# Retention and two feed-forward layers on one core: four edits to who makes the decay table, when the second layer's weights are rounded, and the order of the hand-over between the layers

## The chip, the cores and the metric

The kernel runs on one core of one Trainium2 chip. The metric is the device time of the program in microseconds; the median of the runs is compared. Five engines matter here: TensorE (PE for its matmuls, PEld for the loading of their weights), VectorE (DVE), ScalarE (ACT), GpSimd (POOL), and SyncE (SP), which only issues transfers. Each runs its own instructions in order, and waits for the others by semaphores.

## The reference

All is in float32. With 4 batches, 8 heads, 576 positions and 64 columns a head:

```
scores = scale * q @ k.T
ret    = scores * gamma[h] ** (i - j)   where i >= j, else 0
x      = ret @ v                          # as 2304 tokens x 512
h      = x @ w_in                         # 512 x 2048
P      = a0 + a1*h + a2*h^2 + a3*h^3
Q      = 1 + |b0|*|h| + |b1|*h^2
y      = (P / (Q + 1e-6)) @ w_out         # 2048 x 512
h2     = y @ w2_in
out    = (s * relu(h2)^2 + b) @ w2_out
```

## The kernel before, in words

**Numbers.** The products of the two layers are made of rounded operands (fp32r): each operand is split in a high part and the rest, and each product is three matmuls (`three`, L435): high x low, low x high, high x high.

**Retention** (`retention`). 16 pairs of heads are walked in a hand-written order. For a pair p the loop does, on TensorE: `value_state(p)` (L301), `state(p + 1)` (L289), `value_chunk(p)` (L309) and `scores(p + 2)` (L274). Around them ScalarE copies the state (L292), VectorE adds to it (L293), masks the scores (L278), and multiplies the result by the decay table `odec` (L312); ScalarE and GpSimd split the product x into `xh` and `xl`. The two `pv` tiles in PSUM alternate, so `state(p + 1)` writes where x of pair p - 1 was read from. GpSimd scales v of pair p + 3 (L256). The inputs come over SP's queue, five pairs ahead. The table `odec` has four head pairs; its first 128 columns are loaded, and `decay` (L249) makes the other 448 from them by three multiplications with a power of gamma a row: columns 128, 256 and 64 wide. It is called for head pair 0 at the start, and for 1 to 3 in the loop's rounds 1 to 3.

**Weights.** One tile `raw{kf}` (1 MB, loaded over SP's queue) holds a block of w_in and of w_out, as 64-bit numbers. It is rounded by `w_round`: one ScalarE instruction (`wm`, L139) and three of VectorE (L140, L142, L145), and split by `w_split` (ScalarE's cast of the high part, GpSimd's subtraction for the low). In the retention the first three tiles are rounded step by step (L177 to L185). There are 16 tiles a layer (numbers 0 to 15 and 16 to 31), and only a few buffers: from tile 15 on two `raw` buffers alternate, so a tile is loaded when the one two before it has had its last reader. For layer two, GpSimd also makes four sums of two tiles (`s_sums`, L635 to L638), which are then split (`s_split`, L646 and L588) and written to DRAM.

**Layer one** is cut in 72 units, numbers 0 to 71. A unit has its own h (one PSUM bank, 12 matmuls of 512 columns, or 24 of 256), then `rational` (L481): a chain of some six ScalarE, five VectorE and two GpSimd instructions that ends in the split gate `gh` and `gl` (or `gx`, for both), then its output product `o` (12 matmuls, L525). `emit_cuts` puts the rounding of tiles 3 to 15 between units; tiles 16 and 17, the first of layer two, are rounded by `first_cuts` (L920), one step a unit, from the unit at which `free_at[NF - W_BUFS + 1]` is reached.

**Layer two** is done in quads of two tiles (`quad`). The first quad of a pass has four full products (`hs00`, `hs01`, `hs11`, `hs10`, and a tail `ht`); the others use seven products of block sums in place of eight. The sums of token blocks are made by GpSimd's adding transfers (`x_sum`, L603) and split by `x_split` (L612, L588). Output products of the quad before (`p`, `out2`) are taken from a list between the products by `fill(n)`. The first contribution of each is copied from PSUM to `acc` (L726), by VectorE and ScalarE in turn; later ones are added by VectorE (L728).

**What sets the order.** In the retention every instruction is pinned in the order of the code. In the layers a scheduler sets each engine's order at build time; `behind(...)` holds an instruction back until those named have been issued, and `fill` sets how many output products stand between two products.

Of the kernel before, what the change touches and what calls it, by code (L numbers as in the profile page):

```python
# [14 lines left out]
AF = mybir.ActivationFunctionType  # L15
ALU = mybir.AluOpType
# [13 lines left out]
W_BUFS = 5  # L30
# [9 lines left out]
W_FIRST = 3  # L40
# [4 lines left out]
def retention_ffn_kernel(ctx, tc, a, b, s2, b2, w, qkv, maskv, gdec, out):  # L45
    nc = tc.nc
# [5 lines left out]
    NF = w.shape[0] // 2  # L52
# [30 lines left out]
    w_raw = {}  # L83
# [13 lines left out]
    def next_load(eng=nc.sync, pin=free):  # L97
        if w_ahead:
            loads[:] = loads[-1:] + [w_load(w_ahead.pop(0), eng, pin)]
# [71 lines left out]
    def w_cut_in_halves(kf):  # L171
        pin = tc.keep_in_program_order
        lo, hi = w_words(kf)
        m = wtmp.tile([P, 2 * DM], F32, tag="wm", name=f"wm{kf}")
        t = m.bitcast(U32)
        halves = [slice(DM * x, DM * (x + 1)) for x in range(2)]
        pin(nc.scalar.activation(m, hi.bitcast(F32), AF.Copy, scale=2.0 ** -112))  # L177
        pin(nc.vector.tensor_scalar(lo, lo, 2.0 ** -29, 7.0, op0=ALU.mult, op1=ALU.min))
        yield
        for x in halves:  # L180
            pin(nc.vector.scalar_tensor_tensor(out=t[:, x], in0=t[:, x], scalar=3, in1=lo[:, x],
                                               op0=ALU.logical_shift_left, op1=ALU.bitwise_or))
            yield
        for x in halves:
            pin(nc.vector.scalar_tensor_tensor(out=hi[:, x], in0=hi[:, x], scalar=0x80000000, in1=t[:, x],  # L185
                                               op0=ALU.bitwise_and, op1=ALU.bitwise_or))
            if x.start:
                w_split(kf, True)
                del w_raw[kf]
            yield  # L190
# [6 lines left out]
    def retention(actx):  # L197
# [15 lines left out]
        powers = mv[:, NV:].rearrange("p (k h) -> p k h", k=3)  # L213
# [34 lines left out]

        def decay(hp):  # L249
            for k, (t0, t1) in enumerate(((P, 2 * P), (2 * P, 4 * P), (4 * P, S))):  # L250
                dve(nc.vector.tensor_scalar(odec[:, hp, t0:t1], odec[:, hp, 0:t1 - t0], powers[:, k, hp:hp + 1], None, op0=ALU.mult))

        def scale(p, eng=nc.gpsimd):
            if p < NPAIR:
# [123 lines left out]
                    pass  # L378
        for _ in steps:
            pass  # L380
        next_load()


    def ffn(fctx):
# [66 lines left out]
        NU = len(units)  # L451
# [22 lines left out]
        def behind(*instructions):  # L474

            hold = ExitStack()
            for x in instructions:
                hold.enter_context(tc.issue_after(x.ins))
            return hold
# [227 lines left out]
        def out2(q, j, e, parts=1):  # L707

            t0 = 2048 if j == 2 else 1024 * (q // (NF // 2)) + 512 * j
            es = slice(e * P, (e + 1) * P)  # L710
            k = out_units.setdefault((t0, e), 0)
            n = DM // parts
            for x0 in range(0, DM, n):
                cols = slice(x0, x0 + n)
                ps = ps_o.tile([P, 512], F32, tag="o", name=f"p{16 * q + 4 * j + e}_{x0}")[:, 0:n]
                for i in range(2):
                    if j == 2:
                        g = [x[:, 256 * i:][:, es] for x in gt["q", q, 0, 2]]
                    else:
                        g = [x[:, es] for x in gt["q", q, i, j]]  # L720
                    wf, lf = (t.rearrange("p c f -> p (c f)")[:, cols] for t in w_t[NF + 2 * q + i, 1])
                    for x in three(ps, g, (wf, lf), i == 0, i == 1):
                        pe(x)
                at = acc[:, NC * t0 + e * DM:NC * t0 + (e + 1) * DM][:, cols]
                if k == 0:
                    (nc.vector.tensor_copy if e % 2 else nc.scalar.copy)(at, ps)  # L726
                else:
                    nc.vector.tensor_tensor(out=at, in0=at, in1=ps, op=ALU.add)  # L728
                if k + 1 == NF // 2:
                    nc.sync.dma_start(out=out[t0 + e * P:t0 + (e + 1) * P, cols], in_=at)  # L730
            if e == (3, 3, 1)[j]:
                for i in range(2):
                    g_done(("q", q, i, j))
            out_units[t0, e] = k + 1
# [15 lines left out]
        def quad(q, fills):  # L750
# [49 lines left out]
            if q % (NQ // 2) == 0:  # L800
                while late:
                    late.pop(0)()

                tags = ("hA", "hB", "hG", "hT") if first else ("hA", "hT", "hG", "hB")
                order = ((0, 0), (0, 1), (1, 1), (1, 0)) if first else ((0, 0), (1, 0), (0, 1), (1, 1))
                for n, ((i, j), tag) in enumerate(zip(order, tags)):
                    ps = ps_h.tile([P, 512], F32, tag=tag, name=f"hs{i}{j}")
                    wh, wl = tiles_of(q)[i]
                    for c in range(NC):
                        h, l = both(f"{c // 2 + 1}{j + 1}", pas)  # L810
                        for x in three(ps, (wh[:, c, :], wl[:, c, :]), (h[:, c % 2, :], l[:, c % 2, :]), c == 0, c == NC - 1):
                            pe(x)
                    if not first:
                        split = relu2(("q", q, i, j), ps, True, wait=True)
                        fill((4, 4, 2, 0)[n])
                        done = split()
                    else:
                        done = relu2(("q", q, i, j), ps, True)
                    with behind(*ends, *done):
                        if n == 0:  # L820
                            if first:
                                cut_first()
                            else:
                                x_sum(1, "4")
                        if n == 1 and not first:
                            x_split(pas, "1")
                        if n == (2 if first else 1):
                            x_split(pas, "3")
                    if first:
                        fill(4)  # L830
                    with behind(*ends, *done):
                        if n == 2 and first:
                            x_sum(0, "4")
                            cut_second()
                        if n == 3:
                            with behind(*tail_lo):
                                x_split(pas, "2")
                    ends[:] = done
                if first:
                    tail_in(q)  # L840
                else:
                    with behind(*ends):
                        x_split(1, "4")
                fill(len(fills))
                return
# [3 lines left out]
            last = q == NQ // 2 - 1  # L849

            product(q, 1, hA, True)
            copied = nc.scalar.copy(hB, hA)
            if q == 1:

                with behind(copied):
                    x_split(0, "1")
            while late:
                late.pop(0)()
            n1, n2, n3, n4, n5 = (3, 1, 2, 2, 1) if q == 1 else (2, 2, 2, 2, 1) if first else (2, 1, 1, 2, 2)
            fill(n1)  # L860
            product(q, 2, hA, False)
            split = relu2(("q", q, 0, 0), hA, True, wait=True)
# [52 lines left out]

        sums = ["1", "3", "2", "4"]
        raw_gone = []
        first_rounds = None
        next_cuts = iter(())

        def first_cuts():
            yield from w_round(NF)
            w_split(NF)
            yield
            yield from w_round(NF + 1)

        for u in range(NU):
            emit_in(u)
            if u:
                emit_cuts(u)  # L930
            with behind(*ends):
                next(next_cuts, None)
            rational(u)
            if not items and not cuts and not raw_gone:
                raw_to_g()
                raw_gone.append(u)
            for x in outs_at[u]:
                if x < NU - 3:
                    for e in range(NC):
                        out1(x, e)  # L940
            if final[0:1024].all() and len(sums) > (1 if u == NU - 1 else 2):
                x = sums.pop(0)
                if x in ("1", "3"):
                    x_negate(0, {"1": "11", "3": "22"}[x])
                with behind(*ends):
                    x_sum(0, x)
            if not items and not cuts and first_rounds is None and u + 1 >= free_at[NF - W_BUFS + 1]:
                first_rounds = True
                next_cuts = first_cuts()
        assert first_rounds and sums == ["4"]  # L950
        for _ in next_cuts:
            pass
        rest = [lambda x=x, e=e: out1(x, e, pe) for x in range(NU - 3, NU) for e in range(NC)]
        w_split(NF + 1)
        for x in (NF, NF + 1):
# [90 lines left out]
```

## Time and profile before

| | |
|---|---|
| median of 3 runs | 858.07 us (857.96 to 858.33) |
| the profiled execution | 857.59 us, of which the span of instructions is 855.8 us |
| PE busy | 841.9 us, 98% |
| PEld busy | 713.2 us, 83% |
| DVE busy | 637.6 us, 75% |
| ACT busy | 584.1 us, 68% |
| POOL busy | 397.7 us, 46% |

Times in rows are from the span's start. A row of the timeline has its start, its length, the engine, the line, the operation with its tiles and shapes, how many were merged, and in brackets the engine's idle time before it and what ended that. The retention takes the first 72 us or so, layer one runs to about 473, layer two to the end.

### The profile page before, as it was taken

The page shows a single profiled execution, that of the slowest core. Times are in us where ns is not written, and L with a number is a line of the kernel's source. Part 1 is how long each engine was busy: PE and PEld are TensorE (multiplying, and loading weights), DVE is VectorE, ACT ScalarE, POOL GpSimd, SP SyncE. Part 2 cuts the span into 40 slices and gives each one's busy share as a digit, 9 for nine tenths or more (in the row PEclk, how much of TensorE's full clock was granted, in tenths as well). Part 3 has the DMA queues.
Part 4 walks back from the last instruction along what each step waited for, and adds up shares of the span by engine and source line. Part 5 has one row for each costly group of instructions (what it writes and reads, how often), then busy time and mean ns, then how long its engine had stood idle before and what let it go on. Part 6 is the DMA issues. An engine that isn't in the chain of part 4 may idle for free.

```text
span 855.8 us, 12807 instructions
## 1 busy us (share of the span) xinstructions
PE 841.9 (98%) x4840; PEld 713.2 (83%) x4840; DVE 637.6 (75%) x892; ACT 584.1 (68%) x940; POOL 397.7 (46%) x322
## 2 busy tenths in 40 slices
PE   8999999999999999999999999999999999999998
PEld 7898788888888888888887877888888888888887
DVE  5986887788798879788799977887878554444444
ACT  1236997886787878788789776876668666544443
POOL 3687675465566755557457443442236221111100
PEclk9999999999999999999999999999999999999999
DMA  9992110111102101101003476455779985544302
GB/s 342 402 359 100 49 50 1 50 50 49 50 2 99 50 2 50 49 1 50 2 1 80 118 246 208 152 170 208 246 249 371 244 243 161 158 148 149 123 0 99
DMA packets 39181, 110.79 MB, mean 129 GB/s; under 512 B 3920, under 2 KB 4816, under 8 KB 34128
## 3 DMA queue, kind: packets, MB, share of 16 engines
q1 hardware_dynamic: 28256, 81.67, 27.0%
q0 software_dynamic: 10864, 28.31, 11.7%
q8 instruction: 38, 0.62, 0.3%
q14 instruction: 23, 0.19, 0.1%
HBM read 76.94 MB, written 28.84 MB: 124 GB/s over the span
## 4 chain that ended last, share of the span: by engine, by line
PE 83%; DVE 6%; ACT 4%; DMA 3%; issue 2%; POOL 1%; SPq 0%; ACTq 0%; DVEq 0%; POOLq 0%
PE p L438 21%; PE o L438 19%; PE h L438 18%; PE hB L438 6%; PE hG L438 4%; PE hA L438 4%; PE ht L438 2%; PE sc L274 2%; PE hs L438 2%; DMA raw<-in_w_dram 1%; PE pv L309 1%; DVE xl L588 1%; PE pv L301 1%; PE pv L289 1%; DMA vn<-in_qkv_dram 1%
## 5 line engine op out<-in xcount | busy, mean ns | idle before, releaser
L438 PE MATMUL h<-xh,w 128*128 128x512 f32 (+1 forms) x640 | 184.9, 368 | 0.0
L438 PE MATMUL o<-gh,w 128*128 128x512 f32 (+1 forms) x584 | 165.9, 369 | 0.0
L486 POOL TENSOR_TENSOR tq<-tq,ta 128x512 f32<-128x512 f32 x72 | 98.2, 1364 | 97.4 <-ACT tq L485 94.1
L728 DVE TENSOR_TENSOR acc<-acc,p 128x512 f32<-128x512 f32 (+1 forms) x127 | 86.2, 680 | 71.9 <-PE p L438 70.9
L438 PEld LDWEIGHTS h<-xh,w 128*128 128x128 f32 x640 | 116.3, 188 | 20.4
L438 PE MATMUL p<-w,gh 128*128 128x512 f32 (+1 forms) x338 | 124.3, 388 | 0.0
L438 PEld LDWEIGHTS o<-gh,w 128*128 128x128 f32 x584 | 106.1, 189 | 18.3
L438 PE MATMUL h<-xl,w 128*128 128x512 f32 (+1 forms) x320 | 118.0, 369 | 0.6 <-DVE tt L495 0.6
L498 POOL TENSOR_TENSOR gl<-tt,gh 128x512 fp32r<-128x512 f32 x66 | 93.8, 1423 | 44.4 <-ACT gh L497 33.3
L438 PE MATMUL o<-gl,w 128*128 128x512 f32 (+1 forms) x292 | 108.1, 370 | 2.1 <-POOL gl L498 2.1
L438 PE MATMUL p<-w,gx 128*128 128x512 f32 (+1 forms) x363 | 99.9, 388 | 1.4 <-DVE gx L588 0.7
L163 POOL TENSOR_TENSOR w<-raw,w 128x512 fp32r<-128x512 f32 x32 | 47.7, 1521 | 80.4 <-DMA ss<-xl 27.6
L438 PEld LDWEIGHTS p<-w,gx 128*128 128x128 f32 x363 | 67.7, 188 | 16.3 <-ACT gx L701 1.1
L493 DVE SCALAR_TENSOR_TENSOR tt<-tt,aneg,h 128x512 f32<-128x512 f32 x72 | 53.5, 744 | 31.4 <-ACT h L492 31.3
L438 PEld LDWEIGHTS p<-w,gh 128*128 128x128 f32 x338 | 63.5, 188 | 13.1
L490 ACT ACTIVATE ta<-tq,lnb 128x512 f32<-128x512 f32 x72 | 52.2, 727 | 27.5 <-POOL tq L486 26.9
L488 DVE TENSOR_TENSOR tt<-tt,h 128x512 f32<-128x512 f32 x72 | 49.1, 682 | 27.7 <-ACT tt L487 25.8
L438 PEld LDWEIGHTS h<-xl,w 128*128 128x128 f32 x320 | 60.3, 188 | 11.2 <-DVE tt L495 1.0
L438 PE MATMUL p<-w,gl 128*128 128x512 f32 (+1 forms) x169 | 65.5, 388 | 0.0
L438 PEld LDWEIGHTS o<-gl,w 128*128 128x128 f32 x292 | 55.1, 189 | 12.3 <-POOL gl L498 3.3
L692 ACT ACTIVATE ta<-hG 128x512 f32<-128x512 f32 x14 | 8.4, 598 | 79.4 <-PE hG L438 79.4
L485 ACT ACTIVATE tq<-ta,babs 128x512 f32<-128x512 f32 x72 | 58.9, 818 | 0.2 <-DVE h L494 0.2
(147 smaller groups left out, 1824.7 us busy)
## 6 DMA issues: line engine op xcount, KB each, us to landing
raw<-in_w_dram SPq DMA_DIRECT2D x32, 1024.0 KB, 6.0
ws<-w SPq DMA_DIRECT2D x32, 512.0 KB, 8.4
w<-ws POOLq DMA_DIRECT2D x32, 512.0 KB, 5.6
xT<-in_qkv_dram SPq DMA_DIRECT2D x16, 576.0 KB, 8.0
sf<-ss POOLq DMA_DIRECT2D x7, 1024.0 KB, 5.1
vn<-in_qkv_dram SPq DMA_DIRECT2D x16, 320.0 KB, 7.6
out_dram<-acc SPq DMA_DIRECT2D x17, 256.0 KB, 2.7
kn<-in_qkv_dram SPq DMA_DIRECT2D x16, 256.0 KB, 7.3
```

The source lines that it names most:

```text
L163: nc.gpsimd.tensor_tensor(out=dst[:, 1], in0=src, in1=f32(dst[:, 0]), op=ALU.subtract)
L274: pe(nc.tensor.matmul(ps[j][:, cs], lhsT=xt[r, 0, k0:k0 + P], rhs=xt[r, 1, cs], start=True, stop=True))
L289: pe(nc.tensor.matmul(ps[r, c:c + n, :], lhsT=kn[p][:, c, j, :], start=c == 0, stop=True, rhs=vn[p][:, c, j, :].unsqueeze(1).to_broadcast( ...
L301: pe(nc.tensor.matmul(pv[p][r, cs], lhsT=spre[p % 2][r, c - 1, :], rhs=xT[p][r, 1, cs], start=c in (1, NMAIN), stop=True, skip_group_check ...
L438: yield nc.tensor.matmul(ps, lhsT=lh, rhs=rh, start=start and x == 0, stop=stop and x == 2, skip_group_check=True)
L485: nc.scalar.activation(tq, ta, AF.Identity, bias=babs[:, 0:1], scale=babs[:, 1:2])
L486: nc.gpsimd.tensor_tensor(out=tq, in0=tq, in1=ta, op=ALU.mult)
L488: nc.vector.tensor_tensor(out=tt, in0=tt, in1=h, op=ALU.mult)
L490: nc.scalar.activation(ta, tq, AF.Ln, bias=lnb, scale=QS)
L493: nc.vector.scalar_tensor_tensor(out=tt, in0=tt, scalar=aneg[:, 0:1], in1=r, op0=ALU.add, op1=ALU.mult)
L498: nc.gpsimd.tensor_tensor(out=gl, in0=tt, in1=f32(gh), op=ALU.subtract)]
L728: nc.vector.tensor_tensor(out=at, in0=at, in1=ps, op=ALU.add)
```

## The change

1. `decay` (L249): the three multiplications are ScalarE's `activation` with Copy and a scale a row, in place of VectorE's `tensor_scalar`.
2. The third weight tile (number 2) is no longer split at the end of the retention, but after the first unit's `rational`; the load of a further tile (`next_load`) goes with it.
3. `out2`: all first contributions are copied by ScalarE (9 of 18 were VectorE's).
4. The first quad of layer two: block sums 1 and 3 are split behind its second product, and the first product is no longer followed by output products. In the second quad sum 1 is no longer split, and the numbers of output products between products are 3, 2, 2, 1, 1 in place of 3, 1, 2, 2, 1.
5. `first_cuts`: tiles 16 and 17 are rounded from the first unit after the last of layer one's tiles has been rounded.

```
 def decay(hp):
-                dve(nc.vector.tensor_scalar(odec[:, hp, t0:t1], odec[:, hp, 0:t1 - t0], powers[:, k, hp:hp + 1], None, op0=ALU.mult))
+                pin(nc.scalar.activation(odec[:, hp, t0:t1], odec[:, hp, 0:t1 - t0], AF.Copy, scale=powers[:, k, hp:hp + 1]))
...
 def w_cut_in_halves(kf):
-            if x.start:
+            if x.start and kf < W_FIRST - 1:
...
 def out2(q, j, e, parts=1):
-                    (nc.vector.tensor_copy if e % 2 else nc.scalar.copy)(at, ps)
+                    nc.scalar.copy(at, ps)
...
 def quad(q, fills):
-                        if n == 1 and not first:
+                        if n == 1:
                             x_split(pas, "1")
-                        if n == (2 if first else 1):
                             x_split(pas, "3")
-                    if first:
+                    if first and n:
                         fill(4)
...
-            copied = nc.scalar.copy(hB, hA)
-            if q == 1:
-
-                with behind(copied):
-                    x_split(0, "1")
+            nc.scalar.copy(hB, hA)
...
-            n1, n2, n3, n4, n5 = (3, 1, 2, 2, 1) if q == 1 else (2, 2, 2, 2, 1) if first else (2, 1, 1, 2, 2)
+            n1, n2, n3, n4, n5 = (3, 2, 2, 1, 1) if q == 1 else (2, 2, 2, 2, 1) if first else (2, 1, 1, 2, 2)
...
+        cuts_from = NU
...
+            if u >= cuts_from:
+                with behind(*ends):
+                    next(next_cuts)
             rational(u)
+            if u == 0:
+                w_split(W_FIRST - 1)
+                del w_raw[W_FIRST - 1]
+                next_load()
...
-            if not items and not cuts and first_rounds is None and u + 1 >= free_at[NF - W_BUFS + 1]:
-                first_rounds = True
-                next_cuts = first_cuts()
+            if not items and not cuts and cuts_from == NU:
+                cuts_from = u + 1
```

**ScalarE at the start of the retention.** `spre` is the copied state, `odec` the decay table, `xh` the high part of x, `wm` the first step of a weight tile's rounding. Before:

```order
L292 COPY spre_114<-pv_115 128x128
L314 CAST xh<-x_242 128x576
L292 COPY spre_113<-pv_276 128x128
L314 CAST xh<-x_301 128x576
L292 COPY spre_114<-pv_335 128x128
L314 CAST xh<-x_360 128x576
```

With the change:

```order
L292 COPY spre_114<-pv_115 128x128
L314 CAST xh<-x_242 128x576
L292 COPY spre_113<-pv_276 128x128
L251 ACTIVATE odec<-odec,mv 128x128
L251 ACTIVATE odec<-odec,mv 128x256
L251 ACTIVATE odec<-odec,mv 128x64
L314 CAST xh<-x_301 128x576
L292 COPY spre_114<-pv_335 128x128
L251 ACTIVATE odec<-odec,mv 128x128
L251 ACTIVATE odec<-odec,mv 128x256
L251 ACTIVATE odec<-odec,mv 128x64
L314 CAST xh<-x_360 128x576
```

In each of the rounds 1 to 3 three instructions stand on ScalarE between the state's copy and the cast of x; on VectorE the same three, between the state's sum (L293) and x (L312), are gone.

**VectorE in layer one, first rounding of tile 16.** `tt` is a unit's element-wise tile, `acc` the outputs' sum. Line numbers of layer one are one less in the changed code. Before, the first of the three stood here, at unit 66:

```order
L495 SCALAR_TENSOR_TENSOR tt65_4373<-h65_4358,tt65_4373 128x512
L140 TENSOR_SCALAR raw16_3662<-raw16_3662 128x1024
L489 SCALAR_TENSOR_TENSOR tt66_4423<-tt66_4423,aneg_72,h66_4405 128x512
L488 TENSOR_TENSOR tt67_4467<-tt67_4467,h67_4451 128x512
L489 SCALAR_TENSOR_TENSOR tt67_4467<-tt67_4467,aneg_72,h67_4451 128x512
```

With the change, at units 57 to 59:

```order
L494 SCALAR_TENSOR_TENSOR tt56_3909<-h56_3887,tt56_3909 128x512
L140 TENSOR_SCALAR raw16_3662<-raw16_3662 128x1024
L488 TENSOR_TENSOR tt58_4002<-tt58_4002,aneg_72,h58_3986 128x512
...
L494 SCALAR_TENSOR_TENSOR tt57_3956<-h57_3938,tt57_3956 128x512
L142 SCALAR_TENSOR_TENSOR wm16_3951<-wm16_3951,raw16_3662 128x1024
...
L494 SCALAR_TENSOR_TENSOR tt58_4002<-h58_3986,tt58_4002 128x512
L145 SCALAR_TENSOR_TENSOR raw16_3662<-raw16_3662,wm16_3951 128x1024
L488 SCALAR_TENSOR_TENSOR tt60_4098<-tt60_4098,aneg_72,h60_4080 128x512
```

Both tiles' rounding moves up by some nine units; tile 17's first step now follows unit 59. ScalarE's and GpSimd's part of it moves with it.

**ScalarE in the second quad.** `p` are output products, `tq1` a copy of the fifth product, `gx` a gate's high part, `wm20` the first step of tile 20. Before:

```order
L877 COPY tq1_4981<-hG1_4915 128x512
L139 ACTIVATE wm20_5006<-raw20_4688 128x1024
L695 ACTIVATE hA1_4913<-ta106_4957,b2_sb_75,s2_sb_74 128x512
L726 COPY acc_1119<-p0_0_4983 128x512
L701 CAST gx_3925<-hA1_4913 128x512
L612 CAST xh_79<-acc_1119 128x512 x2
```

With the change:

```order
L725 COPY acc_1114<-p7_0_4961 128x512
L694 ACTIVATE hA1_4917<-ta106_4957,b2_sb_75,s2_sb_74 128x512
L725 COPY acc_1114<-p0_0_4969 128x512
L700 CAST gx_3925<-hA1_4917 128x512
L611 CAST xh_79<-acc_1114 128x512 x2
L871 COPY tq1_4989<-hG1_4919 128x512
L139 ACTIVATE wm20_5014<-raw20_4688 128x1024
L725 COPY acc_1114<-p1_0_4991 128x512
```

The first step of tile 20, which waits for that tile's load, now stands behind the gate's cast in place of ahead of it. Tile 2's instructions (edit 2) stand where they stood on every engine, and SP's order is the same.

## Rows read from the trace of the kernel before

**Rows 1.** The page, busy time, share and instructions of each engine.

```profile
PE 841.9 (98%) x4840; PEld 713.2 (83%) x4840; DVE 637.6 (75%) x892; ACT 584.1 (68%) x940; POOL 397.7 (46%) x322
```

**Rows 2.** The chain that ended last: start, us, what; a unit's matmuls, tile 21's load.

```profile
114.56 2.72 PE h L438 x12
...
500.44 11.88 DMA raw<-in_w_dram
```

**Rows 3.** Timeline of PEld in the retention: start, us, what [idle before <-releaser].

```profile
21.20 0.78 PEld L289 LDWEIGHTS pv<-vn,kn 128*64 128x64 f32 x16 [1.38 <-issue]
...
30.45 0.69 PEld L289 LDWEIGHTS pv<-vn,kn 128*64 128x64 f32 x13 [1.32 <-issue]
```

**Rows 4.** The same from 465 to 521 us, the rows with idle time.

```profile
467.60 0.19 PEld L438 LDWEIGHTS o<-gl,w 128*128 128x128 f32 x1 [2.31 <-POOL gl L498]
492.49 0.19 PEld L438 LDWEIGHTS hA<-xl,w 128*128 128x128 f32 x1 [0.36 <-ACT hB L852]
494.11 0.54 PEld L438 LDWEIGHTS p<-w,gx 128*128 128x128 f32 x3 [0.39 <-DVE acc L726]
497.56 0.19 PEld L438 LDWEIGHTS hG<-xh,xl 128*128 128x128 f32 x1 [2.00 <-DVE xl L588]
506.25 0.19 PEld L438 LDWEIGHTS hG<-xl,xh 128*128 128x128 f32 x1 [0.88 <-DVE hG L880]
518.99 0.19 PEld L438 LDWEIGHTS p<-w,gx 128*128 128x128 f32 x1 [1.13 <-ACT gx L701]
520.22 0.30 PEld L438 LDWEIGHTS p<-w,gx 128*128 128x128 f32 x2 [1.05 <-DVE gx L588]
```

**Rows 5.** Timeline of DVE in the retention, the decay table and x.

```profile
7.92 0.84 DVE L251 TENSOR_SCALAR odec<-odec,mv 128x128 f32<-128x128 f32 x3 [0.93 <-DMA odec<-in_gdec_dram]
...
17.40 2.86 DVE L251 TENSOR_SCALAR odec<-odec,mv 128x128 f32<-128x128 f32 x3
20.36 0.76 DVE L312 TENSOR_TENSOR x<-pv,odec 128x576 f32<-128x576 f32 x1
```

**Rows 6.** Windows: length, busy us (count) of PE, PEld, DVE, ACT, POOL, clock, DMA, GB/s.

```profile
20.00:40.00 20.00, 17.56 (x319) 16.70 (x321) 18.59 (x31) 5.77 (x11) 13.54 (x10) 1.00 1.03 405
...
400.00:440.00 40.00, 40.00 (x218) 34.77 (x217) 32.10 (x48) 29.73 (x51) 22.23 (x17) 1.00 0.00 1
440.00:480.00 40.00, 38.11 (x169) 31.24 (x168) 36.29 (x51) 32.83 (x52) 27.45 (x20) 1.00 0.31 83
465.00:521.00 56.00, 50.64 (x239) 40.83 (x238) 47.66 (x56) 44.23 (x74) 26.95 (x24) 1.00 0.48 141
```

**Rows 7.** ScalarE's copies of the mask: lowest, median and highest ns, first and last start.

```profile
L343 ACT COPY mask<-mv x1: 618/618/618, 2.9 to 2.9; 128x512 f32<-128x512 f32 x1
L344 ACT COPY mask<-mv x1: 239/239/239, 3.4 to 3.4; 128x64 f32<-128x64 f32 x1
```

**Rows 8.** Timeline of POOL in the retention: v of pair 5 is scaled.

```profile
26.17 1.26 POOL L256 TENSOR_TENSOR vn<-vn,mv 128x640 f32<-128x640 f32 x1 [2.85 <-PE pv L289]
```

**Rows 9.** ScalarE's copies of L726, columns as in rows 7.

```profile
L726 ACT COPY acc<-p x9: 562/586/589, 494.0 to 716.9; 128x512 f32<-128x512 f32 x9
```

**Rows 10.** Timeline of VectorE: a rounding step of tile 17, beside GpSimd's work.

```profile
462.90 1.81 DVE L142 SCALAR_TENSOR_TENSOR wm<-wm,raw 128x1024 uint32<-128x1024 uint32 x1
```

**Rows 11.** Timeline from 488 us: the same step of tile 19, and GpSimd's last sum.

```profile
488.22 1.21 DVE L142 SCALAR_TENSOR_TENSOR wm<-wm,raw 128x1024 uint32<-128x1024 uint32 x1
...
494.14 1.12 POOL L638 TENSOR_TENSOR tt<-raw,tt 128x256 f32<-128x256 f32 x1
```

**Rows 12.** Timeline of ACT: tile 20's first step, and the cast of the late gate.

```profile
501.47 1.12 ACT L139 ACTIVATE wm<-raw 128x1024 f32<-128x1024 f32 x1 [1.85 <-DMA raw<-in_w_dram]
...
518.32 0.61 ACT L701 CAST gx<-ta 128x512 fp32r<-128x512 f32 x1
```

**Rows 13.** Timeline of POOL, second adding transfer; DMA issues, 440 to 530 us.

```profile
468.63 0.90 POOL L603 DMA_DIRECT2D acc<-acc  x1 [1.09 <-PE o L438]
...
acc<-acc POOLq DMA_DIRECT2D x4, 512.0 KB, 4.6
```

More of the change, by code (lines that the diff above doesn't have):

```diff
@@ L380, in retention @@
             pass
-        next_load()
     def ffn(fctx):
@@ L917, in ffn @@
         raw_gone = []
-        first_rounds = None
-        next_cuts = iter(())
+        cuts_from = NU
         def first_cuts():
@@ L925, in first_cuts @@
             yield from w_round(NF + 1)
+            while True:
+                yield
+        next_cuts = first_cuts()
         for u in range(NU):
@@ L930, in ffn @@
                 emit_cuts(u)
-            with behind(*ends):
-                next(next_cuts, None)
+            if u >= cuts_from:
+                with behind(*ends):
+                    next(next_cuts)
             rational(u)
+            if u == 0:
+                w_split(W_FIRST - 1)
+                del w_raw[W_FIRST - 1]
+                next_load()
             if not items and not cuts and not raw_gone:
@@ L946, in ffn @@
                     x_sum(0, x)
-            if not items and not cuts and first_rounds is None and u + 1 >= free_at[NF - W_BUFS + 1]:
-                first_rounds = True
-                next_cuts = first_cuts()
-        assert first_rounds and sums == ["4"]
-        for _ in next_cuts:
-            pass
+            if not items and not cuts and cuts_from == NU:
+                cuts_from = u + 1
+                assert cuts_from + 2 >= free_at[NF - W_BUFS] and cuts_from + 6 < NU
+        assert sums == ["4"]
         rest = [lambda x=x, e=e: out1(x, e, pe) for x in range(NU - 3, NU) for e in range(NC)]
```

## The prediction

> **What bounds the kernel now.** The page comes first: PE is busy 841.9 us, 98% of the span, and no other engine comes near [rows 1]. So nothing is gained by making another engine's work shorter; what can go is PE's idle time, some 14 us. Next, the chain that ended last: a unit's 12 matmuls take 2.72 us [rows 2], and that pace is the yardstick for how far a piece of PE work moves when one group is put ahead of it. Then the timeline of PEld, since a matmul that must wait shows as its weight load's idle time. Two waits stand in the retention [rows 3], seven between 465 and 521 us [rows 4]; I found no other of a microsecond inside the layers. Their sum is 1.38 + 1.32 + 2.31 + 0.36 + 0.39 + 2.00 + 0.88 + 1.13 + 1.05 = 10.82 us. Each is costed by itself, against the profiled execution's 857.59 us, 0.48 below the median of 858.07.
>
> **Edit 1, the table.** The state's matmuls start at 21.20 after an idle 1.38 that the view puts down to "issue". Their real hindrance is on VectorE: the three multiplications run from 17.40 to 20.26, x follows from 20.36 to 21.12, and the state, which writes the bank that x has read, starts 0.08 later [rows 3, 5]. PE was ready at 21.20 - 1.38 = 19.82, so x must end by 19.74, and start by 18.98. The same three took 0.84 us at 7.92 [rows 5]; at 17.40 they stretch, and in 20 to 40 us VectorE is busy 18.59 of 20 us, ScalarE 5.77 [rows 6]. ScalarE's price is not in the trace for this form. Its copies take 618 ns for 512 columns and 239 for 64 [rows 7], which makes 0.85 ns a column and 0.18 us besides, so 0.29, 0.40 and 0.24 for 128, 256 and 64 columns: 0.93 us a pair. That is the low bound. If ScalarE were stretched as VectorE is (2.86/0.84 = 3.4 times) it would be 3.2, the table would be late by 0.3 more, and the edit would cost 0.6 over two rounds. I take 0.93, because the mask rows are this engine's own and of the same shape. The table is then done by 17.40 + 0.93 = 18.33, at least 0.6 ahead of 18.98. Both waits go: **-2.70**. What is queued behind the three on ScalarE is the cast of x, which waits for x in any case. Late next is the input: v of pair 5 is scaled by 26.17 + 1.26 = 27.43 [rows 8]; its state starts at 30.45 now and at 27.75 without the waits, 0.3 to spare.
>
> **Edit 2, the third tile's split.** Its instructions stand where they stood on every engine, and SP's order too: 0.
>
> **Edit 3, the copies.** Nine more on ScalarE, 0.586 each: 5.3 us in all [rows 9], taken from VectorE. Between 465 and 521 us ScalarE is busy 44.23 of 56 us, VectorE 47.66 [rows 6], so it evens them out. No copy is a PE product's input; it only frees a bank. 0 by itself; without the cover, up to 0.59 at each copy that a product waits for, and the 0.39 at 494.11 is such a wait [rows 4].
>
> **Edit 5, rounding sooner.** Six VectorE steps, two ScalarE steps and the splits leave 440 to 474 us, where VectorE is busy 36.29 of 40 us, for some 391 to 440, where it has 40 - 32.10 = 7.9 us free and no load is under way (1 GB/s), so the tiles are there [rows 6]. Beside GpSimd a step takes 1.81, alone 1.21 [rows 10, 11]: the move is 7.3 to 10.9 us of work (six steps, the first of each tile at most as long). Taking that out of the crowded stretch lets unit 69's gate, for which PE waits 2.31 at 467.60 [rows 4], be made on time; with the output of unit 69 placed one group (2.72) later in the new order besides, that wait goes: **-2.31**. Everything behind it on VectorE comes up to 6 us sooner: tile 19's rounding, and with it the sums of blocks, whose last now ends at 494.14 + 1.12 = 495.26 [rows 11]. By the new order I put that at about 489.
>
> **Edit 4, the hand-over.** The 2.00 at 497.56 is PE waiting for the low part of a block sum [rows 4]. With the sums at 489 that low part is there at about 490.6; by counting PE's groups in the new order it is wanted at 494.3. The 0.36 and 0.39 in front are queues at a bank, and ease with the copies: **-2.75** together, of which I give back 0.36 for the ordinary gaps. The 0.88 at 506.25 starts on ScalarE: tile 20's first step waits 1.85 for that tile's load, until 501.47, and the gate's cast and the casts of x stand behind it [rows 12]. In the new order it stands behind them, and the load, freed by the sums, is sooner too: **-0.88**. The last two, 1.13 and 1.05, are for a gate that ScalarE casts at 518.32 [rows 4, 12], behind the rounding of tile 21, whose load takes from 500.44 to 512.32 [rows 2]. With sums sooner by 6 it lands at about 506, the gate's low part is there at 511.5 to 512, and PE wants it at 513.1: **-2.18**, with only about 1 us to spare.
>
> **Sum.** 857.59 - 2.70 - 2.31 - 2.75 - 0.88 - 2.18 = 846.77. I add back the 0.36 and 0.4 for small new waits (the order leaves margins of 0.3 to 1 us in four places, and each 0.36 or 0.39 above is what such a miss costs), which makes 847.5. With 0.48 to the median: **848.0 us**.
>
> **Rivals.** *The third and fourth stalls stay.* Tile 21's load needs 11.88 us because it stands behind six stores on SP's queue; if the sums come only 3 us sooner, the load lands at 509, the gate is ready after 513.1, and 0.88 and 2.18 are kept, with the copies now on ScalarE ahead of that gate. Less 7.75: 857.59 - 7.75 + 0.48 = 850.3. For it: the thin 1 us. Against it: the work that leaves ScalarE's and VectorE's path ahead.
>
> *The input stream bounds the retention.* In 20 to 40 us the transfers move 405 GB/s at a share of 1.03 [rows 6]; if pair 5's v can't come sooner, what is gained at x is lost 0.3 us later, and with 2.70 kept it is 850.7. Against it: the state of pair 5 would then have to use up all of those 0.3 us, and most rounds show no such wait. The Trainium skill (Perfetto Trace Analysis, Roofline) says that a single core is bounded by its 16 DMA engines, at about 435 GB/s; the trace agrees so far, with 405. By that figure a pair's 1152 KB (worked out from its tiles' shapes) would be, as an estimate, 2.7 us, under a round's 4, so the stream would catch up.
>
> *Earlier rounding overfills VectorE.* At 1.81 a step the six are 10.9 us against 7.9 free: 3.0 too many, and layer one's gates then come late by that: 847.5 + 3.0 + 0.48 = 851.0. For it: the stretch beside GpSimd [rows 10, 11]. Against: GpSimd is busy only 22.23 of those 40 us [rows 6], and the first steps of the two are the short ones. The Trainium skill (GPSIMD Engine Reference, 1. Specifications) says that GpSimd shares its SBUF interfaces with VectorE, and that instructions with two SBUF inputs contend; these steps have two, and 1.81 against 1.21 agrees. If that rule held for every step it is this rival's case; if for none, the forecast's.
>
> *Slower.* The casts of block sums 1 and 3 now stand on ScalarE right behind the second product of the first quad, at about 472 us, and wait for the second adding transfer, which GpSimd issues at 468.63 now and which takes 4.6 us [rows 13]. With the 2.31 gone I put the issue at about 465 to 467 and its landing at 470 to 472: a margin of 0 to 2. If instead GpSimd's queue held the issue for another six groups of PE (16 us), ScalarE would be held 13 us and every gate behind it, PE with it, for all but a group or so: 847.5 + 12 + 0.48 = 860 and more, say 862. It decides only from a landing after about 484; for it there is nothing in the present order of that queue.
>
> *The gain comes back elsewhere*: the waits move to the next group and only 1 us is won: 857.
>
> **Chances.** Forecast 0.57, third and fourth stalls 0.20, input stream 0.07, VectorE overfilled 0.06, slower 0.04, given back 0.06. The range 846.4 to 852.5 holds the first four: below, all of the waits gone with the 0.76 that I gave back; above, one of the rivals with a small wait more. About 0.2% (1.7 us) is what a measurement of this kernel can tell from no change. Faster by more than that (below 856.4) takes in the first four: 0.90. Within it the last: 0.06. Slower: 0.04.
>
> **What the profile after would show.** Edit 1: rounds of the retention all about 4 us long, no PEld wait near 20 or 28. Edit 5: no wait of 2 us for unit 69's gate; PE 40.00 busy of 400 to 440 still. Edit 4: the last sum ends near 489 (less what the retention gained), tile 20's load lands 6 us sooner, and no wait of 1 us behind it. Wrong would be: the state of pair 5 or 6 waiting for v; a wait at the first quad's second gate with ScalarE idle for an adding transfer; or 1 to 2 us waits for gates at the second quad's end.

## The result and the profile after

The changed kernel takes 848.45 us (median of 4 runs, 848.11 to 849.61), the kernel before 858.02 beside it: a ratio of 0.989, 95% interval 0.9873 to 0.9908. Forecast were 848.0 us, 846.4 to 852.5, and 0.90 for faster. The profiled execution has a span of 846.4 us in place of 855.8. One run of edit 1 alone (1120.41 us) and one of the last version (1709.04) took far longer than the other runs of the same kernel; the figures below leave both out, and as the first is the one that was profiled, edit 1 alone has no trace of its waits.

The page's busy times, and the waits of PEld by what they wait for (us in total, times, longest):

```profile
PE 840.5 (99%) x4840; PEld 713.9 (84%) x4840; DVE 618.0 (73%) x871; ACT 593.8 (70%) x961; POOL 397.3 (47%) x322
```

```profile
PEld pv L326 <- DVE expb L970: 1.1, 1, 1.1
PEld h L437 <- DVE tt L494: 1.0, 1, 1.0
PEld o L437 <- POOL gl L497: 1.0, 2, 0.6
PEld pv L289 <- POOL vn L256: 0.8, 1, 0.8
PEld sc L274 <- DVE pm L278: 0.4, 1, 0.4
PEld pv L301 <- DVE raw L185: 0.4, 1, 0.4
PEld p L437 <- DVE gx L587: 0.3, 1, 0.3
```

Against [rows 1] the span is 9.4 us shorter and PE is busy 1.4 less: 8.0 of it is idle time that went (13.9 before, 5.9 now), the rest is in PE's busy time, of which the ends of matmuls are modelled. VectorE lost 19.6 us and ScalarE gained 9.7, mostly by edits 1 and 3. All nine waits of [rows 3, 4] are gone but for 0.3 us before `gx`. The waits at the very start, at the retention's end and of layer one's first units (`expb`, `pm`, `raw`, `tt`, two of `gl`) were there before. One is new: 0.8 us for `vn` in the retention.

The two places again, in PEld's timeline of the changed kernel (start, us, what, idle before): the state's matmuls of the rounds that waited in [rows 3], the new wait, and what is left of [rows 4].

```profile
19.50 0.75 PEld L289 LDWEIGHTS pv<-vn,kn 128*64 128x64 f32 x16
23.48 0.75 PEld L289 LDWEIGHTS pv<-vn,kn 128*64 128x64 f32 x16
27.47 0.75 PEld L289 LDWEIGHTS pv<-vn,kn 128*64 128x64 f32 x16
...
48.18 0.75 PEld L289 LDWEIGHTS pv<-vn,kn 128*64 128x64 f32 x16 [0.84 <-POOL vn L256]
...
510.73 0.30 PEld L437 LDWEIGHTS p<-w,gx 128*128 128x128 f32 x2 [0.26 <-DVE gx L587]
```

The rounds are 3.98 us apart with no idle time. The windows, columns as in [rows 6], show PE without a gap where the rounding of tiles 16 and 17 went, and across the hand-over:

```profile
391.00:440.00 49.00, 49.00 (x262) 42.48 (x262) 45.38 (x71) 42.07 (x69) 35.18 (x26) 1.00 0.15 49
...
465.00:521.00 56.00, 56.00 (x270) 46.99 (x269) 41.25 (x52) 48.34 (x82) 23.97 (x21) 1.00 0.55 161
```

VectorE is at 45.38 of 49 us there: nearly full, but PE does not notice. At the hand-over it fell from 47.66 to 41.25, PE rose from 50.64 to 56.00. In GpSimd's timeline the last of the sums, and on ScalarE the casts that the "slower" rival feared:

```profile
464.44 0.91 POOL L602 DMA_DIRECT2D acc<-acc  x1 [1.21 <-DMA acc<-acc]
469.33 0.87 POOL L602 DMA_DIRECT2D acc<-acc  x1 [0.75 <-DMA acc<-acc]
...
486.94 0.75 POOL L637 TENSOR_TENSOR tt<-raw,tt 128x256 f32<-128x256 f32 x1
```

```profile
470.10 2.18 ACT L611 CAST xh<-acc 128x512 fp32r<-128x512 f32 x4
```

The sums end at 487.69 in place of 495.26 [rows 11]. The second adding transfer was issued at 464.44; the third, which waits for a transfer of `acc` to land, was issued at 469.33. So the second had landed by then, some 0.8 us before the casts that wait for it (1.1 us by the 4.6 us of [rows 13]).

### The profile page after: what moved, and what is told of

It reads as the page before. It is cut to its first block, busy times and chain, and to the rows that moved or that the text cites. A ratio compares the mean times of both kernels' runs of the same rounds, so it can differ in the third digit from the quotient of the medians.

```text
span 846.4 us, 12801 instructions
## 1 busy us (share of the span) xinstructions
PE 840.5 (99%) x4840; PEld 713.9 (84%) x4840; DVE 618.0 (73%) x871; ACT 593.8 (70%) x961; POOL 397.3 (47%) x322
## 4 chain that ended last, share of the span: by engine, by line
PE 91%; DMA 4%; POOL 2%; ACT 1%; issue 1%; DVE 0%; SPq 0%; ACTq 0%; POOLq 0%; DVEq 0%
PE p L437 23%; PE o L437 23%; PE h L437 21%; PE hB L437 7%; PE hA L437 5%; PE hG L437 4%; PE ht L437 3%; PE hs L437 3%; DMA vn<-in_qkv_dram 2%; DMA xT<-in_qkv_dram 1%; DMA kn<-in_qkv_dram 1%; PE sc L274 1%; PE pv L289 1%; PE pv L309 1%; PE pv L301 1%
```

## The experiments

**One edit undone at a time**, four kernels of four runs each beside one another on one chip. The changed kernel was not among them: the differences are against its 848.45 us, which a later measurement gave again. The kernel before took 857.26 us beside these four and 857.9 to 858.1 beside the others, so a difference of less than some 0.8 us can't be told from none here.

*Edit 1 undone.*

```
-                pin(nc.scalar.activation(odec[:, hp, t0:t1], odec[:, hp, 0:t1 - t0], AF.Copy, scale=powers[:, k, hp:hp + 1]))
+                dve(nc.vector.tensor_scalar(odec[:, hp, t0:t1], odec[:, hp, 0:t1 - t0], powers[:, k, hp:hp + 1], None, op0=ALU.mult))
```

> The changed kernel with edit 1 undone (the decay table's three multiplications on VectorE again). Theory: the two waits of the retention come back (1.38 and 1.32 us), and the new 0.84 us wait for v at 48.18 us goes with them, since the rounds are then slower than the input stream: 848.4 + 2.3 = 850.7 us (850 to 851.5), and VectorE's multiplications end about 0.1 us behind the GpSimd instruction that they overlap. Rival (the input stream paces the retention anyway): within 0.8 us of the changed kernel, 848.4 to 849.2.

Measured: 850.85 us (850.60 to 851.07), 2.4 above the changed kernel; as the theory had it. PEld's two waits are back, at 25.35 (1.50) and 31.05 (1.76), and no wait for `vn` stands near 48 us. The timeline of VectorE and GpSimd (start, us, engine, line):

```profile
17.34 0.83 DVE L251 TENSOR_SCALAR odec<-odec,mv 128x128 f32<-128x128 f32 x3
18.51 1.27 POOL L256 TENSOR_TENSOR vn<-vn,mv 128x640 f32<-128x640 f32 x1 [3.17 <-DMA vn<-in_qkv_dram]
...
21.43 2.96 DVE L251 TENSOR_SCALAR odec<-odec,mv 128x128 f32<-128x128 f32 x3
21.45 1.27 POOL L256 TENSOR_TENSOR vn<-vn,mv 128x640 f32<-128x640 f32 x1 [0.30 <-DMA vn<-in_qkv_dram]
22.67 1.40 POOL L315 TENSOR_TENSOR xl<-x,xh 128x576 fp32r<-128x576 f32 x1
```

In the round where GpSimd is idle the table takes 0.83 us; where GpSimd runs two instructions back to back, until 24.07, it ends at 24.39. GpSimd's first starts when v lands, so a round's loss hangs on when that transfer lands: here the tables of rounds 2 and 3 are stretched, before it was those of rounds 1 and 3.

*Edit 5 undone* (`first_cuts` starts where it did before; edit 2 is kept).

```
-            if not items and not cuts and cuts_from == NU:
-                cuts_from = u + 1
...
+            if not items and not cuts and first_rounds is None and u + 1 >= free_at[NF - W_BUFS + 1]:
+                first_rounds = True
+                next_cuts = first_cuts()
...
```

> The changed kernel with edit 5 undone (tiles 16 and 17 rounded late, as before). Theory: the 2.3 us wait for unit 69's gate comes back, and with the sums of blocks some 6 us late again also most of the 2.00, 0.88 and 2.18 of the hand-over: 848.4 + 2.3 to 7.4, so 851 to 856, most likely 854.5 us. Rival (edit 4's order removes the hand-over's waits by itself): only the first wait comes back, 850.7 us.

Measured: 852.14 us (851.37 to 853.62), +3.7, between the 854.5 and the 850.7 expected, and the first wait did not come back as expected. PEld has no wait for unit 69's gate; it waits two microseconds for tile 17:

```profile
469.41 0.19 PEld L437 LDWEIGHTS hs<-xl,w 128*128 128x128 f32 x1 [0.77 <-ACT w L162]
471.02 0.30 PEld L437 LDWEIGHTS hs<-xh,w 128*128 128x128 f32 x2 [1.42 <-POOL w L163]
...
513.85 0.19 PEld L437 LDWEIGHTS p<-w,gx 128*128 128x128 f32 x1 [0.71 <-ACT gx L700]
514.71 0.30 PEld L437 LDWEIGHTS p<-w,gx 128*128 128x128 f32 x2 [0.67 <-DVE gx L587]
```

Edit 4 puts the first quad's second product one group earlier, and that product needs tile 17's split. So edit 4's order wants the early rounding; without it the lost time changes its name from `gl` to `w`. The late gate comes back by 1.4 us besides. The 2.00 and the 0.88 do not come back, though the last sum ends only at 491.80 (491.05 + 0.75): that part of the rival holds.

*Edit 4 undone* (the splits of block sums 1 and 3, `fill(4)` behind the first product, fills 3, 1, 2, 2, 1, as before).

```
-                        if n == 1:
+                        if n == 1 and not first:
                             x_split(pas, "1")
+                        if n == (2 if first else 1):
                             x_split(pas, "3")
-                    if first and n:
+                    if first:
                         fill(4)
...
```

> The changed kernel with edit 4 undone (block sums 1 and 3 split where they were before, four output products behind the first product, fills 3, 1, 2, 2, 1). Theory: edit 5 brings the sums early by itself, but two casts and two subtractions of the second quad stand again ahead of what PE wants: one or two waits of 0.4 to 1 us come back, 849.5 to 851 us. Rival A (edit 5 alone clears the hand-over): 848.4 us within 0.4. Rival B (edit 4 is what clears it): 853.5 us.

Measured: 848.55 us (848.27 to 848.71). Rival A: with edit 5 in, edit 4 is worth nothing that the time shows. In the hand-over PEld has one wait of 0.3 us or more, what is left of the 2.31 for unit 69's gate:

```profile
463.35 0.19 PEld L437 LDWEIGHTS o<-gl,w 128*128 128x128 f32 x1 [0.36 <-POOL gl L497]
```

In the changed kernel one more product stands ahead of this unit's output, and that rest is gone; here in turn the 0.26 us before `gx` is gone.

*Edit 3 undone.*

```
-                    nc.scalar.copy(at, ps)
+                    (nc.vector.tensor_copy if e % 2 else nc.scalar.copy)(at, ps)
```

> The changed kernel with edit 3 undone (9 of the 18 first copies on VectorE again). Theory: no product waits for a copy, so 848.4 us within 0.4. Rival: VectorE's 0.68 us copies in the second quad delay the low part of a gate by one copy, 849 to 849.6 us.

Measured: 849.80 us (849.29 to 849.99), +1.35. PEld waits 1.16 and 0.68 us for the late gate at 511.72. That is more than a copy, and it is not VectorE. ScalarE's timeline here, and then that of the changed kernel:

```profile
509.96 1.19 ACT L162 CAST w<-raw 128x512 fp32r<-128x512 f32 x2
511.06 0.61 ACT L700 CAST gx<-ta 128x512 fp32r<-128x512 f32 x1
```

```profile
509.03 0.61 ACT L700 CAST gx<-ta 128x512 fp32r<-128x512 f32 x1
509.54 1.22 ACT L162 CAST w<-raw 128x512 fp32r<-128x512 f32 x2
```

The gate's cast stands behind tile 21's two casts (1.19 us) with the copies alternating, ahead of them with all copies on ScalarE. The scheduler changed the order of two instructions that the edit does not name; tile 21's load lands at about the same time in both (505.6 and 505.2). It is so in every trace that can be compared: with the copies alternating (the kernel before, edit 5 alone, edit 4 alone) the gate's cast stands behind tile 21's two, with all copies on ScalarE (edits 4 and 5 undone) ahead of them.

**One edit alone on the kernel before**, with its lines of the change's diff and no others. Edit 5:

> The kernel before with edit 5 alone (tiles 16 and 17 rounded sooner). Theory (the rounding is what moves the hand-over): unit 69's 2.31 goes, the sums come some 6 us sooner, and with them 2.00 and 0.88 go; the waits for the gate at 519 stay about 1.8 us, since the copies alternate: 858.0 - 2.3 - 2.75 - 0.9 - 0.4, so 851.7 us (851 to 852.8). Rival (rounding and the new order need each other): only the first wait goes, 855.7 us.

Measured: 852.14 us (851.13 to 852.58), -5.8. Of [rows 4] two waits are left, 0.36 of the 2.31 and 0.96 of the late gate: the rounding by itself clears most of the hand-over.

```profile
465.40 0.19 PEld L438 LDWEIGHTS o<-gl,w 128*128 128x128 f32 x1 [0.36 <-POOL gl L498]
...
513.76 0.30 PEld L438 LDWEIGHTS p<-w,gx 128*128 128x128 f32 x2 [0.96 <-DVE gx L588]
```

Edit 4:

> The kernel before with edit 4 alone (the order of the hand-over), tiles 16 and 17 rounded late. Theory, from the run with the rounding late: unit 69's wait goes, but the early product of the first quad then waits some 2 us for the split of tile 17, and the sums come a few us sooner as two block sums are split elsewhere: 855 to 857 us. Rival (edit 4 is worth nothing or harms without the rounding): 858 to 859.5 us.

Measured: 856.37 us (854.43 to 858.02 in 10 runs; ratio 0.9981, interval 0.997 to 0.9991), -1.5, in the theory's range. In the profiled run, the one of 854.43, PEld waits for the split of tile 17 (1.4 and 0.7), for `acc` (0.8) and for the late gate (1.80 and 0.56):

```profile
PEld p L438 <- ACT gx L701: 1.8, 1, 1.8
...
PEld hs L438 <- POOL w L163: 1.4, 1, 1.4
...
PEld ht L438 <- DVE acc L512: 0.8, 1, 0.8
PEld hs L438 <- ACT w L162: 0.7, 1, 0.7
```

The 2.31, 0.36, 0.39, 2.00 and 0.88 of [rows 4] are gone here too, although the last sum ends at 492.87 and not at 489:

```profile
492.12 0.75 POOL L638 TENSOR_TENSOR tt<-raw,tt 128x256 f32<-128x256 f32 x1
```

So the waits for the sums and behind tile 20 have two cures, the early rounding and the new order. What the order alone wins there it loses in part to tile 17.

Edit 1:

> The kernel before with edit 1 alone (the decay table on ScalarE). Theory (the edits' terms add, this one is 2.4 us): 855.6 us (855 to 856.3). Rival (without the rest, the later waits take it back): 857 to 858.

Measured: 855.47 us (854.52 to 857.96 in nine runs; ratio 0.9974, interval 0.9962 to 0.9987): -2.6 by the medians, -2.2 by the ratio. The time falls in the theory's range and below the rival's; the interval, 1.1 to 3.3 us, does not fix the size.

**Edit 2 made real.** On every engine it moved nothing. Here the split is held back until the first unit's gate has been issued:

```
             if u == 0:
-                w_split(W_FIRST - 1)
+                with behind(*ends):
+                    w_split(W_FIRST - 1)
```

> The changed kernel with the split of the third weight tile held back until the first unit's gate has been issued, so that edit 2 does what its words say: ScalarE's 1.17 us cast and GpSimd's two subtractions no longer stand ahead of the first unit's chain. Theory: the waits at 83.95, 86.97 and 92.89 us (0.99, 0.40, 0.56) are the first chain being late; they shrink by 1 to 1.9 us: 846.5 to 847.5. Rival: the order of all units shifts with it and a later wait takes its place, 848.4 or more.

Measured: 851.72 us (851.62 to 851.79), +3.3: the rival. The 0.99 us wait is gone, but the split now stands in the next units' way: where the first units waited 0.99, 0.40 and 0.56 us, they now wait 0.43 and 1.89. The scheduler set other orders at the hand-over as well, 400 us later, and brought back waits there (1.31 for `acc`, 0.69 and 1.15 for the late gate):

```profile
PEld o L437 <- POOL gl L497: 1.9, 1, 1.9
PEld ht L437 <- DVE acc L511: 1.3, 1, 1.3
PEld p L437 <- DVE gx L587: 1.1, 1, 1.1
```

**The new wait for v.** In the retention's loop the two steps that fill GpSimd's queue change places:

```
+            scale(p + 3)
             for _ in range((p > 2) + (p > 13)):
                 next(steps, None)
-            scale(p + 3)
```

> The changed kernel with GpSimd scaling v of pair p + 3 ahead of a weight tile's rounding step instead of behind it, which moves pair 10's v ahead of the first tile's two subtractions. Theory: the new wait of 0.84 us at 48.18 is a GpSimd queue (v had landed at 43.55, 3.3 us before it was scaled), so it goes: 847.6, with no wait near 48 us. Rival (the input stream sets this wait): it stays, 848.4.

Measured: 847.19 us (846.95 to 847.54). The wait is gone: pair 10's v is now scaled by 45.69, and the matmuls that want it start at 48.45. GpSimd's timeline in the changed kernel, then in this one:

```profile
40.78 1.26 POOL L256 TENSOR_TENSOR vn<-vn,mv 128x640 f32<-128x640 f32 x1 [2.69 <-DMA vn<-in_qkv_dram]
42.01 1.88 POOL L315 TENSOR_TENSOR xl<-x,xh 128x576 fp32r<-128x576 f32 x1
43.89 3.02 POOL L158 TENSOR_TENSOR w<-raw,w 128x512 fp32r<-128x512 f32 x2
46.86 1.26 POOL L256 TENSOR_TENSOR vn<-vn,mv 128x640 f32<-128x640 f32 x1
```

```profile
44.44 1.25 POOL L256 TENSOR_TENSOR vn<-vn,mv 128x640 f32<-128x640 f32 x1
45.66 3.00 POOL L158 TENSOR_TENSOR w<-raw,w 128x512 fp32r<-128x512 f32 x2
```

GpSimd waits 2.69 us for pair 9's v, which the input stream brings late, and then has the low part of x (1.88) and the low parts of the first tile's split (3.02) ahead of pair 10's v, whose user is PE at 48.18. Both belong to it: the stream makes the queue late, the queue makes PE wait. How long PE waits changes from execution to execution: with the same code for the retention it was 0.84, 0.83, 0.74, 0.35, 0.29 and nothing in six traces (the changed kernel twice, edits 5, 4 and 3 undone, the split held back). So a trace without the wait is not proof by itself; that v now comes 2.8 us ahead of PE is the better sign.

Again, beside the changed kernel on one chip:

> The changed kernel itself, beside the next on one chip: 848.4 us, with the wait for v near 48 us between 0 and 0.84.

> The version in which GpSimd scales v ahead of the rounding step, again, beside the changed kernel on one chip: 847.2 us, 1.0 to 1.4 below it. Rival (the difference was the chip's): within 0.4 of it.

Measured: 848.45 us (848.21 to 848.61) for the changed kernel, with 0.74 us of waiting near 48 us, and 847.17 (847.09 to 848.01 in three runs) for the other, whose trace has no wait there. That is 1.3 us by the medians, as in the theory, and 1.0 by the ratios to the kernel before (0.9887, 0.987 to 0.9904, and 0.9875, 0.9855 to 0.9896). The two intervals overlap, but much of their width is the kernel before (856.45 to 859.85); the runs of the two versions themselves do not overlap. With so few runs the size stays rough. It is the fastest version run.

**What stretches VectorE.** The table on VectorE again, in a form of the instruction that also sums each row:

```
+        dsum = sb1.tile([P, 1], F32, name="dsum")
...
-                pin(nc.scalar.activation(odec[:, hp, t0:t1], odec[:, hp, 0:t1 - t0], AF.Copy, scale=powers[:, k, hp:hp + 1]))
+                dve(nc.vector.tensor_scalar(odec[:, hp, t0:t1], odec[:, hp, 0:t1 - t0], powers[:, k, hp:hp + 1], None, op0=ALU.mult, op1=ALU.add, accum_out=dsum))
```

> The decay table on VectorE as in the first experiment, with a form of the same multiplication that also writes the sum of each row. Theory: the stretch of the plain form (1.27 and 1.39 us in place of 0.29 and 0.35) is VectorE waiting for a pair of ports that GpSimd's instruction holds to its end, and the accumulating form does not ask for these ports: each of the three then takes the same time in every round (0.3 to 0.6 us, about 1.2 to 1.5 a table), the two waits of 1.5 and 1.8 us at 25 and 31 us shrink to under 0.3 us each, and the time is 848 to 849 us. Rival (VectorE is stretched by any work of GpSimd's): a table still takes over 2 us in two rounds, 850.5 to 851.5.

Measured: 848.39 us (848.24 to 849.22), no different from the table on ScalarE. Two instructions of the plain form (edit 1 undone), each by itself, in the round in which GpSimd is at work:

```profile
21.43 1.37 DVE L251 TENSOR_SCALAR odec<-odec,mv 128x128 f32<-128x128 f32 x1
22.83 1.39 DVE L251 TENSOR_SCALAR odec<-odec,mv 128x256 f32<-128x256 f32 x1
```

In the round at 17.34, where GpSimd is idle, the same two take 0.28 and 0.35. The groups by shape of the summing form (busy, mean ns):

```profile
L253 DVE TENSOR_SCALAR_CACHE_REDUCE odec<-odec,mv 128x256 f32<-128x256 f32 x4 | 1.9, 479 | 0.1
L253 DVE TENSOR_SCALAR_CACHE_REDUCE odec<-odec,mv 128x128 f32<-128x128 f32 x4 | 1.4, 338 | 0.9 <-DMA odec<-in_gdec_dram 0.9
```

and two of its instructions in the same round, with GpSimd's timeline:

```profile
21.43 0.34 DVE L253 TENSOR_SCALAR_CACHE_REDUCE odec<-odec,mv 128x128 f32<-128x128 f32 x1
...
21.81 0.48 DVE L253 TENSOR_SCALAR_CACHE_REDUCE odec<-odec,mv 128x256 f32<-128x256 f32 x1
```

```profile
21.47 1.26 POOL L258 TENSOR_TENSOR vn<-vn,mv 128x640 f32<-128x640 f32 x1 [0.32 <-DMA vn<-in_qkv_dram]
22.69 1.41 POOL L317 TENSOR_TENSOR xl<-x,xh 128x576 fp32r<-128x576 f32 x1
```

Beside the same GpSimd instructions as in edit 1 undone, the summing form takes 0.34 and 0.48 us, as in the other rounds, and a table is done in 1.2. The plain form took 2.96, some 2 us more than where GpSimd is idle. The waits of 1.50 and 1.76 us are gone; one of 0.47 for the table is left at 26.13. The stretch is a matter of the instruction's form, not of VectorE being slow beside GpSimd: the rival falls. The Trainium skill (SBUF — State Buffer, Who interferes with whom) has the rule: `tensor_scalar`, "not the form that also writes out its accumulator", can run in a mode that takes the port pair which VectorE shares with GpSimd, and the later of the two waits for the whole of the other's instruction. These two forms agree with it. On the order the trace says less: the first of the two stretched instructions starts at 21.43, 0.02 us before GpSimd's, and yet it is the one that is held.

## Why the prediction was right, and where it was not

The total was right: 848.0 against 848.45. Of 10.82 us of waits 0.26 are left and 0.84 are new, so 9.7 went; the prediction had kept 0.76. The measured difference is 9.6. Its terms were less well placed, and that the total fits so closely is in part luck: of the 2.18 for the late gate 1.84 still stand when edit 3, which was put at 0, is undone.

| step | predicted | undone in the changed kernel | alone on the kernel before |
|---|---|---|---|
| edit 1, decay on ScalarE | -2.70 | +2.4 | -2.2 to -2.6 |
| edit 2 | 0 | not run; made real, +3.3 | not run |
| edit 3, copies | 0 | +1.35 | not run |
| edit 5, rounding | -2.31, and the sums sooner | +3.7 | -5.8 |
| edit 4, hand-over | the rest, with edit 5 | +0.1 | -1.5 |

*Edit 1.* The releaser was read rightly, behind the view's "issue". The size came out some 0.3 too large: undone, waits of 1.50 and 1.76 come back and 0.84 goes, 2.4 net. The table costs more than estimated, by ScalarE's groups in the changed kernel:

```profile
L251 ACT ACTIVATE odec<-odec,mv 128x256 f32<-128x256 f32 x4 | 2.0, 509 | 0.1
L251 ACT ACTIVATE odec<-odec,mv 128x128 f32<-128x128 f32 x4 | 1.6, 402 | 0.3 <-DMA odec<-in_gdec_dram 0.3
L251 ACT ACTIVATE odec<-odec,mv 128x64 f32<-128x64 f32 x4 | 1.3, 332 | 0.0
```

0.51, 0.40 and 0.33 in place of 0.40, 0.29 and 0.24: 1.18 us (the three overlap a little). The state's wait vanished all the same. What takes part of the gain back is "late next is the input": right in kind, wrong in place. Pair 5's v, for which 0.3 to spare was forecast, came in time (there at 27.00, wanted at 27.47); pair 10's, behind a late pair 9 and a tile's split, did not, and costs 0.84. That rival, priced at 2.7, was true for at most a third.

*Edit 2*: put at 0, as its instructions stand where they stood; no run undoes it alone.

*Edit 3* is the step that failed. "No copy is a PE product's input; it only frees a bank. 0 by itself" counts what the copies take, 0.59 each. It left out that the scheduler sets ScalarE's whole order anew: the cast of the late gate comes ahead of tile 21's two casts, not behind them, and that is worth 1.35 (1.16 + 0.68 of waiting for the gate in place of 0.26).

*Edit 5 and edit 4.* The prediction gave 2.31 to the rounding with the order besides, and 2.75, 0.88 and 2.18 to sums that come sooner with both. The runs show two cures for the same waits. The rounding alone leaves 0.36 of the 2.31 and 0.96 of the late gate, and clears the rest; the order alone clears the 2.31 and the waits around the sums too, but pays 2.1 to tile 17 and keeps 2.4 of the late gate. So behind edit 5 there is next to nothing left for edit 4. The 0.36 and 0.39 were to ease with the copies, but they are gone with the copies alternating too. For the 0.88 both ways can be seen. With edit 4 undone tile 20's step stands ahead of the gate's cast as before, but the load lands at 494.3 in place of 501.4; with edit 4 alone the load lands late, at 499.2, but the step stands behind the cast (496.02), as the prediction had it.

*The late gate.* "Only about 1 us to spare" was the right warning: tile 21's load lands at 505.2 where, less the retention's 2.7, 503.3 was expected, and the gate's low part misses by 0.26. With the copies as before PE waits 1.16 and 0.68 for it (0.96 behind edit 5 alone): sooner sums by themselves do not win the 2.18. That half of the rival "the third and fourth stalls stay" (0.20) would mostly have held without edit 3, though not for its reason, a load at 509; its other half, the 0.88, would not.

*VectorE overfilled.* The six steps moved were put at 7.3 to 10.9 us; from 388.56 to 413.51 they took 1.21 + 1.22 + 1.60 + 1.67 + 1.22 + 1.54 = 8.46. VectorE is at 45.38 of 49 there, and PE at 49.00. The rival falls, though with not much room.

*Slower.* The adding transfer landed some 0.8 to 1.1 us ahead of the casts, in the 0 to 2 expected.

## What to carry to other kernels

Where a scheduler sets each engine's order, an edit is not worth what its instructions take: read the order of the instructions that wait last, on the engine that they share, before giving an edit 0. When several edits aim at one stall, undo each by itself and run each alone: two may be cures for the same wait, and then undoing one shows nothing. And after a wait has gone, look at the queue that feeds the next one: here two neighbours on GpSimd had only to change places.

## What the runs showed of the hardware that was not expected

A VectorE `tensor_scalar` of 0.28 or 0.35 us took 1.37 or 1.39 beside GpSimd, and ended about 0.1 us after GpSimd's instruction did. A form of the same operation that also writes a sum was not held at all: 0.34 and 0.48 us in every round, with 0.08 us more for the reading of each sum. So the edit had an equal alternative without a change of engine: 848.39 against 848.45 us.

Which rounds are hit, and how hard, changes from execution to execution with the landing of a transfer. With the table on VectorE the retention's waits for the state were 1.38 and 1.32 us (at 21.20 and 30.45) in the kernel before, 1.50 and 1.76 (25.35 and 31.05) with edit 1 undone, 1.54 and 1.13 with edit 5 alone, and 0.36, 0.51 and 0.75 with edit 4 alone. A price read from one trace, 2.70 here, stands for 1.6 to 3.3.
